# Thirteen chunks' combined weights finished ahead and kept in DRAM, and the first Strassen tile's x split on GpSimd: attention and two gated FFNs on one core

## The chip, the core and the metric

One core of a Trainium2 chip. The engines are TensorE (PE, whose weight loads are PEld), VectorE (DVE), ScalarE (ACT), GpSimd (POOL) and SyncE (SP); here SP issues nearly all DMAs, in one queue, in order. The metric is the device time of one launch in microseconds (us).

## What is computed

```python
B, H, S, D = 4, 8, 576, 64          # 2304 tokens of 512
scores = where(mask, q @ k.T / 8, -1e9)   # heads 0-3: the last 32 keys; heads 4-7: every 32nd key
x = softmax(scores) @ v             # 2304 x 512
xn = x / sqrt(mean(x * x) + 1e-6) * rms_g
x = (silu(xn @ w1_gate) * (xn @ w1_val)) @ w1_out     # d_ff 1536
out = (silu(x @ w2_gate) * (x @ w2_val)) @ w2_out
```

The six weight matrices come as 64-bit floats, 512x1536 or 1536x512.

## The kernel before

**Numbers.** A float64 weight block ("raw", 512 KB of 32-bit words, L211) is made into fp32 on the chip: two ACT steps (L228 low word, L220 high word) and two DVE steps (L232, L237). Every matrix product is then made of three fp32r products (hi x hi, hi x lo, lo x hi), so each operand is split: an ACT cast gives hi (L244 for weights, L1024 for x), a subtraction gives lo (DVE L248 for weights, L1025 for x).

**Two stages.** The hidden dimension is cut into 12 chunks of 128 in each FFN. Stage A (to about 396 us) does the attention and chunks 0 to 5 of the first FFN ("plain", six token segments of 256 to 512 tokens; functions `gate`, `hidden`, `down`). Stage B does chunks 6 to 11 of the first FFN and all of the second in five passes: chunks (6,7,8), (9,10,11), then (0-3), (4-7), (8-11). Each pass walks three supertiles of 768 tokens; gate and value products of a chunk are one 2x2 Strassen-Winograd product, of seven matrix products in place of eight.

**Strassen's operands.** For each supertile x is loaded (`stage_x`), and POOL forms four sums (L1008) and seven lo parts (L1025), two halves each. For the weights of a chunk `combined_step` (L268) loads gate and value blocks, decodes both, lets POOL form four differences of 128x256 (`sums`, L283, written into the raw buffer), and splits four parts into hi and lo.

**Places and order.** A finished chunk takes three of the 4 KB-per-partition places in `room[4]` and one 2 KB place in `room[2]`; there are three raw buffers. The list `late` holds the weight steps of stage B in order. `prefetch` starts the next one when its places are free, and `weights` lets `pace["op"]` of its operations go out at each point of the main program. Every engine runs its instructions in the order in which a scheduler issues them; `behind("act")` (L313) puts a weight operation behind the last ACT instruction of the main chain.

**The ACT chain of stage B.** Of the seven products the epilogue copies some from PSUM by ACT: `keep` (L1053, tile t), `seed` (L1059), silu (L1067); DVE adds (L1063, L1073), and ACT casts the hidden value (L1077). PE's next product goes into the bank that `keep` or `seed` has just emptied. At the end of stage A the program runs `plainpiece` (the last two down products) among the first Strassen products, and before that it stages the first supertile with `sum_x` and `split_q` on DVE.

Of the kernel before, what the change touches and what calls it, by code (L numbers as in the profile page):

```python
# [8 lines left out]
F32 = mybir.dt.float32  # L9
# [12 lines left out]
PRIO_W = -150  # L22
# [3 lines left out]
def attn_ffn_ffn(ctx: ExitStack, tc: tile.TileContext, q, k, v, w1g, w1v, w1o, rms_g, w2g, w2v, w2o, out):  # L26
# [58 lines left out]
    wq = []  # L85
    state = {"start": True, "hold": False, "kind": "", "lag": 3, "wait": 4}
# [41 lines left out]
    def prefetch(force=False):  # L128
        if late and (late[0].ready() or force) and not wq:
            st = late.pop(0)  # L130
            phase(st, 0)
            st.at, st.lag = clock[0], state["wait"]
            begun.append(st)
# [19 lines left out]
    def point():  # L153
        advance()
        weights()
# [45 lines left out]
    raws = [3]  # L201

    def fetch(m, c, z):
        raws[0] -= 1
# [5 lines left out]
        r = dec.tile([128, KC, 256], U32, tag="raw", name="raw", bufs=3)  # L210
        nc.sync.dma_start(out=r, in_=src)  # L211
        words = r.rearrange("p k f -> p (k f)").rearrange("p (n s) -> p n s", s=2)
        return {"raw": r, "lw": words[:, :, 0], "hw": words[:, :, 1]}

    def scale(cell, free=1):

        def high():
            cell["h"] = dec.tile([128, 512], F32, tag="dh", name="dh")
            with behind("act"):
                nc.scalar.activation(out=cell["h"], in_=cell["hw"].bitcast(F32), func=AF.Copy, scale=2.0 ** -112)  # L220

# [28 lines left out]
    def weight_step(m, c, z):  # L250
        cell = {}

        def load():
            cell["at"] = take((m, c, z == 2), 4)
            cell.update(fetch(m, c, z))
# [10 lines left out]
        return Step([load] + scale(cell) + [first, second], lambda: room[4] and raws[0] >= 1, PRIO_W)  # L266

    def combined_step(m, c):  # L268

        g, v = {}, {}  # L270
        at = []

        def load():
            at.extend([take((m, c, False), 4) for _ in range(3)] + [take((m, c, False), 2)])
            g.update(fetch(m, c, 0))
            v.update(fetch(m, c, 1))

        def sums():
            t = g["raw"].rearrange("p k f -> p (k f)").bitcast(F32).rearrange("p (a n) -> p a n", a=4)
# [4 lines left out]
            flat = t.rearrange("p a n -> p (a n)")  # L284
            g["parts"] = [(g["h"], 512, at[0]), (v["h"][:, 256:512], 256, at[3]), (flat[:, 0:512], 512, at[1]), (flat[:, 512:1024], 512, at[2])]
            g["t"] = []

        def first(i):
            def f():
                src, w, place = g["parts"][i]  # L290
                t = home(place, w, f"w{m}_{c}_{i}")
                g["t"].append(t)
                hi(t, src)
            if i == 2:
                f.late = True
            return f

        def second(i):
            def f():
                lo(g["t"][i], g["parts"][i][0])  # L300
                if i == 3:
                    raws[0] += 1
                    tg, tb, t12, t34 = g["t"]
                    wt[m, c, 0] = {1: tg[:, :, 0:256], 2: tg[:, :, 256:512], 3: tb, 5: t12[:, :, 0:256], 6: t12[:, :, 256:512],
                                   7: t34[:, :, 0:256], 4: t34[:, :, 256:512]}
                    wdone.add((m, c, 0))
            return f

        return Step([load] + scale(g, 0) + scale(v) + [sums] +
                    [f(i) for i in range(4) for f in (first, second)],  # L310
                    lambda: len(room[4]) >= 3 and room[2] and raws[0] >= 2, PRIO_W)

# [563 lines left out]

    segs = [(1, *e, 0, HC) for e in early]
# [17 lines left out]
    for key in (1, 0):  # L895
# [8 lines left out]
    late += [combined_step(1, c) if z == "c" else weight_step(1, c, 2) for z, c in  # L904
             (("c", 6), ("c", 7), ("d", 6), ("c", 8), ("d", 7), ("d", 8), ("c", 9), ("d", 9), ("c", 10), ("d", 10), ("c", 11), ("d", 11))]
    late += [combined_step(2, c) if z == "c" else weight_step(2, c, 2) for z, c in
# [38 lines left out]

    for si, (m, t0, n, c0, c1) in enumerate(segs):
        nxt = segs[si + 1] if si + 1 < len(segs) else None
# [6 lines left out]
        for c in range(c0, c1):  # L954
# [6 lines left out]
            if att and not steps and not active_att():  # L961
# [3 lines left out]
                open_pool("x7", "x7", 0, bufs=1)  # L965
                open_pool("wpb", "wpb", 0, bufs=1)
                open_pool("ob", "ob", 512, bufs=4)
                room[4] += [(pools["wpb"][0], f"v{i}") for i in range(2)]
# [19 lines left out]
    HN = 384  # L988
# [7 lines left out]
    xq = {}  # L996
# [194 lines left out]
    for n, (m, cs, t0) in enumerate(work):  # L1191
# [51 lines left out]
        pace["op"] = 1.0 if m == 2 else 0.7 if n else 1.4  # L1243
# [7 lines left out]
        for i, c in enumerate(chunks[:-1]):  # L1251
# [9 lines left out]
            if i == k - 2:  # L1261
                pace["op"] = 0.35 if n else 1.2
# [61 lines left out]
```

## Time and profile before

| what | value |
|---|---|
| three runs, us | 1048.94, 1049.05, 1049.20 (median 1049.05) |
| profiled execution, us | 1045.34 |
| its span, us | 1043.6 |
| mean granted TensorE clock | 0.974 |
| PE / PEld / DVE / ACT / POOL busy, us | 986.6 / 898.8 / 577.7 / 576.2 / 447.4 |
| DMA, MB | 133.85 |

Busy time is summed over the span, whatever the engine's stage; a row "idle before <- releaser" says how long an engine stood and what its wait ended with. Times of rows are from the start of the span. A matmul's own duration overlaps its neighbours': the pace of PE is seen in the distance of starts.

### The profile page before, as it was taken

The numbers are of one execution on the slowest core, as the hardware profiler recorded it, in microseconds if no ns is written. First come the engines' busy times: TensorE is split into PE (matmuls) and PEld (weight loads), VectorE is DVE, ScalarE is ACT, GpSimd is POOL, SyncE is SP. The second block draws the span as 40 slices with busy tenths as digits, with TensorE's granted clock in tenths as the row PEclk, the third lists the DMA queues.
The fourth block names the chain that finished last, engine by engine and source line by source line (L and its number), as shares of the span: only waits on it lengthen the run. The fifth ranks groups of instructions, "written<-read, shape, count | busy, mean of one in ns | idle before, by whom it ended". The sixth has DMA issues, their size and how long they took to land.

```text
span 1043.6 us, 16443 instructions
## 1 busy us (share of the span) xinstructions
PE 986.6 (95%) x5804; PEld 898.8 (86%) x5804; DVE 577.7 (55%) x1311; ACT 576.2 (55%) x1435; POOL 447.4 (43%) x463
## 2 busy tenths in 40 slices
PE   5758999999999997999999999999989999999998
PEld 4648998788789886899999999999988999899997
DVE  3779445454353677644766467433766337663433
ACT  5888646545623567555556467454766346563531
POOL 3312102103100061865696594743848164844500
PEclk9658999999999999999999999999999999999999
DMA  7675242251132256535736534403374342615021
GB/s 188 168 225 149 67 135 75 75 136 35 41 101 91 86 177 216 156 107 162 232 102 211 182 105 166 161 1 122 122 241 138 115 143 71 224 49 182 33 80 61
DMA packets 130090, 133.85 MB, mean 128 GB/s; under 512 B 41428, under 2 KB 113820, under 8 KB 130008
## 3 DMA queue, kind: packets, MB, share of 16 engines
q1 hardware_dynamic: 129816, 132.53, 39.9%
q8 instruction: 45, 0.74, 0.3%
q0 software_dynamic: 192, 0.28, 0.1%
q14 instruction: 37, 0.30, 0.1%
HBM read 99.75 MB, written 33.03 MB: 127 GB/s over the span
## 4 chain that ended last, share of the span: by engine, by line
PE 68%; POOL 10%; DVE 7%; DMA 7%; issue 4%; ACT 3%; SPq 1%; POOLq 0%; DVEq 0%; ACTq 0%
PE b_y L66 27%; PE b_a L66 15%; PE b_g L66 12%; PE b_v L66 11%; POOL xl L1025 5%; POOL raw L283 2%; PE b_a L69 2%; DMA raw<-in_moe_w_out_dram 2%; DVE w L248 2%; POOL xst L1008 1%; DMA raw<-in_moe_w_val_dram 1%; DMA raw<-in_moe_w_gate_dram 1%; DVE dh L237 1%; ACT dh L220 1%; SPq L383 1%
## 5 line engine op out<-in xcount | busy, mean ns | idle before, releaser
L1025 POOL TENSOR_TENSOR xl<-xst,xh 128x384 fp32r<-128x384 f32 x168 | 177.0, 1083 | 68.1 <-PE b_y L66 36.7
L66 PE MATMUL b_y<-xh,w 128*128 128x384 f32 x700 | 189.3, 336 | 5.5 <-ACT t L1053 5.5
L66 PE MATMUL b_g<-xh,w 128*128 128x384 f32 (+2 forms) x496 | 149.6, 349 | 7.2 <-ACT t L1053 4.5
L66 PEld LDWEIGHTS b_y<-xh,w 128*128 128x128 f32 x700 | 128.1, 188 | 9.0 <-ACT t L1053 7.1
L66 PE MATMUL b_v<-xh,w 128*128 128x384 f32 (+2 forms) x432 | 128.4, 347 | 4.3 <-ACT b_v L1059 2.7
L66 PE MATMUL b_a<-xh,w 128*128 128x384 f32 (+2 forms) x460 | 125.6, 336 | 0.8 <-ACT t L1053 0.7
L66 PE MATMUL b_y<-hh,w 128*128 128x256 f32 (+2 forms) x432 | 117.2, 342 | 1.0 <-ACT hh L800 1.0
L66 PE MATMUL b_y<-xl,w 128*128 128x384 f32 x350 | 117.7, 336 | 0.0
L66 PEld LDWEIGHTS b_g<-xh,w 128*128 128x128 f32 x496 | 91.7, 193 | 15.5 <-ACT t L1053 6.1
L1024 ACT CAST xh<-xst 128x384 fp32r<-128x384 f32 x180 | 85.9, 521 | 23.6 <-POOL xst L1008 20.4
L543 POOL TENSOR_TENSOR e<-e,rc 128x384 f32<-128x384 f32 (+3 forms) x40 | 38.0, 955 | 132.3 <-DVE rc L537 75.5
L283 POOL TENSOR_TENSOR raw<-dh 128x256 f32<-128x256 f32 x36 | 32.7, 928 | 141.6 <-DVE dh L237 106.3
L66 PEld LDWEIGHTS b_v<-xh,w 128*128 128x128 f32 x432 | 78.1, 188 | 12.6 <-ACT b_v L1059 3.5
L66 PEld LDWEIGHTS b_a<-xh,w 128*128 128x128 f32 x460 | 83.4, 188 | 5.1 <-ACT t L1053 1.3
L66 PE MATMUL b_g<-xl,w 128*128 128x384 f32 (+2 forms) x248 | 84.5, 341 | 2.6 <-POOL xl L1025 2.6
L66 PEld LDWEIGHTS b_y<-hh,w 128*128 128x128 f32 x432 | 77.2, 189 | 7.2 <-ACT hh L800 1.4
L66 PE MATMUL b_a<-xl,w 128*128 128x384 f32 (+2 forms) x230 | 77.2, 336 | 0.0
L66 PE MATMUL b_y<-hl,w 128*128 128x256 f32 (+2 forms) x216 | 72.6, 336 | 0.2 <-DVE hl L801 0.2
L66 PE MATMUL b_v<-xl,w 128*128 128x384 f32 (+2 forms) x216 | 72.6, 336 | 0.0
L1008 POOL TENSOR_TENSOR s<-xst 128x384 f32<-128x384 f32 x28 | 29.4, 1071 | 90.7 <-DMA xst<-y_d 53.6
L526 ACT ACTIVATE e<-e,nb 128x96 f32<-128x96 f32 (+2 forms) x152 | 56.3, 373 | 20.3 <-DVE nb L517 20.2
L66 PEld LDWEIGHTS b_y<-xl,w 128*128 128x128 f32 x350 | 65.8, 188 | 1.8
(204 smaller groups left out, 2195.7 us busy)
## 6 DMA issues: line engine op xcount, KB each, us to landing
xst<-y_d SPq DMA_DIRECT2D x18, 768.0 KB
raw<-in_moe_w_gate_dram SPq DMA_DIRECT2D x24, 512.0 KB
raw<-in_moe_w_val_dram SPq DMA_DIRECT2D x24, 512.0 KB
raw<-in_moe_w_out_dram SPq DMA_DIRECT2D x24, 512.0 KB
part<-ob SPq DMA_DIRECT2D x48, 256.0 KB
ob<-part SPq DMA_DIRECT2D x36, 256.0 KB
ob<-part SPq DMA_DIRECT2D x32, 192.0 KB
part<-ob SPq DMA_DIRECT2D x24, 192.0 KB
```

The costliest lines, as they stand in the source:

```text
L66: traced(nc.tensor.matmul(out_, a, b_, start=start, stop=stop, **how))
L69: traced(nc.tensor.transpose(out_, a, one))
L220: nc.scalar.activation(out=cell["h"], in_=cell["hw"].bitcast(F32), func=AF.Copy, scale=2.0 ** -112)
L237: nc.vector.scalar_tensor_tensor(out=h, in0=h, scalar=3, in1=cell["r"], op0=ALU.logical_shift_left, op1=ALU.bitwise_or)
L248: nc.vector.tensor_tensor(out=t[:, 1], in0=src, in1=t[:, 0].bitcast(F32), op=ALU.subtract)
L283: nc.gpsimd.tensor_tensor(out=t[:, z], in0=a, in1=b, op=ALU.subtract)
L383: engs[h].dma_start(out=t[0:108, h].rearrange("p (g d) -> p g d", d=D), in_=s)
L526: r = nc.scalar.activation(out=e[:qn, i, :kn], in_=e[:qn, i, :kn], func=AF.Exp, bias=nb[:qn, i:i + 1], scale=-1.0, accum_out=sums[:qn, i:i ...
L543: eng.tensor_tensor(out=e[:qn, :nt, :kn], in0=e[:qn, :nt, :kn], in1=rc[:qn, :nt].unsqueeze(2).to_broadcast([qn, nt, kn]), op=ALU.mult)
L1008: eng.tensor_tensor(out=out_[:, kk], in0=a[:, kk], in1=b[:, kk], op=op)
L1024: nc.scalar.copy(out=xh[:, kk], in_=src[:, kk])
L1025: eng.tensor_tensor(out=xl[:, kk], in0=src[:, kk], in1=xh[:, kk].bitcast(F32), op=ALU.subtract)
```

## The change

**Parking.** Thirteen of the eighteen chunks of stage B (first FFN 9, 10, 11; second 0, 1, 2, 3, 5, 6, 7, 9, 10, 11) are decoded, combined and split in their raw and "dh" buffers, without a place: hi parts go into the value block's dead raw buffer, lo parts over their sources. Each of the four parts is then stored to DRAM (two DMAs a part, eight a chunk), and the chunk is read back with four DMAs when its places are free. The last cast of a parked chunk overwrites the buffer that its first store reads. Chunks 6, 7, 8 of the first FFN and 4, 8 of the second go the old way. All of a chunk's stores and loads are on SP: 596 rows on that queue stand against 421, and 13 chunks write 23.9 MB and read 23.9 MB (1.835 MB each way a chunk).

**Where parks run.** Parks use the attention stage's three raw buffers at first, so that the parks of chunks 9 and 10 of the first FFN start in the first token segment; between the end of the attention and the last segment a pool "st" gives five raw and five dh buffers.

**First x.** `first_x` stages the first supertile in 128x384 pieces in 14 DMAs (3 before), and issues its 22 sums and lo parts one by one during the last plain segment, on POOL (before: 22 on DVE).

**Paces.** `pace["op"]` in stage B was 1.0 for the second FFN, 0.7 for the first, 1.4 for the first supertile, and 0.35 or 1.2 from the last chunk but one on; it becomes 0.6 (1.0, then 0.8, in the first supertile).

```diff
-    def combined_step(m, c):
+    def combined_step(m, c, how):
...
         def sums():
-            t = g["raw"].rearrange("p k f -> p (k f)").bitcast(F32).rearrange("p (a n) -> p a n", a=4)
+            flat = g["raw"].rearrange("p k f -> p (k f)").bitcast(F32)
+            t = flat.rearrange("p (a n) -> p a n", a=4)
...
+            spaces = v["raw"].rearrange("p k f -> p (k f)").bitcast(F32)
+            src = {0: g["h"], 1: flat[:, 0:512], 2: flat[:, 512:1024], 3: b22}
+            his = {0: spaces[:, 0:512], 1: spaces[:, 512:1024], 2: spaces[:, 0:512], 3: v["h"][:, 0:256]}
+            for i in (0, 3, 1, 2) if how != "park" else (0, 1, 3, 2):
...
+        def save(qs, a, hi_, lo_, t_):
+            w = 256 * len(qs)
+            d = dp.tile([128, 2, w], F32, name=f"pk{m}_{c}_{t_}")
+            nc.sync.dma_start(out=d[:, 0], in_=hi_.bitcast(F32))
+            nc.sync.dma_start(out=d[:, 1], in_=lo_.bitcast(F32))
+            parked.setdefault((m, c), {})[t_] = d
...
+    def recall_step(m, c):
+        def load():
+            got = {}
+            for i, qs in enumerate(QUARTERS):
+                w = 256 * len(qs)
+                t = home(take((m, c, False), 4 if w == 512 else 2), w, f"w{m}_{c}_{i}")
+                nc.sync.dma_start(out=t.bitcast(F32), in_=parked[m, c][i])
...
+        return Step([load], lambda: len(parked.get((m, c), ())) == 4 and len(room[4]) >= 3 and room[2], PRIO_W)
...
-    late += [combined_step(1, c) if z == "c" else weight_step(1, c, 2) for z, c in
-             (("c", 6), ("c", 7), ("d", 6), ("c", 8), ("d", 7), ("d", 8), ("c", 9), ("d", 9), ("c", 10), ("d", 10), ("c", 11), ("d", 11))]
...
+    plan("p19 p110 c16 d16 c17 c18 d17 d18 r19 d19 r110 d110 p111 p20 r111 d111 p21 r20 d20 r21 d21 p22 p23 r22 d22 r23 d23 "
+         "c24 d24 p25 p26 p27 r25 d25 r26 d26 r27 d27 c28 d28 p29 p210 p211 r29 d29 r210 d210 r211 d211")
...
+    def first_x():
...
+            def g():
...
+                with behind("act"):
+                    nc.scalar.copy(out=h[i][:, kk], in_=f[nm, kk])
+                nc.gpsimd.tensor_tensor(out=l[i][:, kk], in0=f[nm, kk], in1=h[i][:, kk].bitcast(F32), op=ALU.subtract)
...
     for si, (m, t0, n, c0, c1) in enumerate(segs):
+        if nxt_last(si):
+            while begun:
+                operate(begun[0])
+            racks.pop(0)
+            close_pools("st")
+            open_pool("x7", "x7", 0, bufs=1)
+            first_x()
...
-    cell = stage_x(1, 0)
-    sum_x(cell, nc.vector)
-    for i in (1, 2, 6, 5, 7, 4, 3):
-        split_q(cell, i, 0, nc.vector)
-        split_q(cell, i, 1, nc.vector)
...
-        pace["op"] = 1.0 if m == 2 else 0.7 if n else 1.4
+        pace["op"] = 0.6 if n else 1.0
...
-                pace["op"] = 0.35 if n else 1.2
+                pace["op"] = 0.6 if n else 0.8
```

In the plan "c" is a chunk combined as before, "p" one that is parked, "r" its recall, "d" the chunk's down weight (loaded and split as before). PE's order is the same, instruction for instruction, but for the weight tiles' names. Three places of the other engines' order follow (line numbers differ between the two programs: L1053 and L1210 are both `keep`, L244 and L251 the cast of a plain weight, L358 that of a combined one).

ACT in the second FFN's first supertile, around the copies t of one gate bank; `w_2_*` and `w_3_*` are weights of chunks 2 and 3 of that FFN. Before:

```order
L1067 ACTIVATE t_6964<-b_v 128x384
L244 CAST w_2_2_6970<-raw 128x512
L1053 COPY t_6975<-b_g 128x384
L220 ACTIVATE dh<-raw 128x512
L244 CAST w_2_3_6988<-raw 128x512
L1053 COPY t_7016<-b_g 128x384
L244 CAST w_3_0_7019<-dh 128x512
L1059 COPY b_a_7029<-b_a_7021 128x384
```

After:

```order
L1224 ACTIVATE t_7141<-b_v 128x384
L1210 COPY t_7150<-b_g 128x384
L251 CAST w_3_2_7166<-dh 128x512
L1210 COPY t_7187<-b_g 128x384
L1216 COPY b_a_7197<-b_a_7190 128x384
L1224 ACTIVATE b_g<-b_g 128x384
L1234 CAST hh<-b_g 128x384
```

Between the two copies the decode step into dh and the cast of raw are gone, and one cast of a down weight stands there.

POOL in the first supertile of the pass over chunks 9, 10, 11 (s is a sum of the next x, raw<-dh the weights' differences, xl the lo parts). Before:

```order
L1025 TENSOR_TENSOR xl<-s_5428,xh 128x384 x2
L283 TENSOR_TENSOR raw<-dh,raw 128x256
L1025 TENSOR_TENSOR xl<-xst,xh 128x384
L1008 TENSOR_TENSOR xst<-xst 128x384
L1025 TENSOR_TENSOR xl<-xst,xh 128x384 x5
L283 TENSOR_TENSOR raw<-dh,raw 128x256
L1025 TENSOR_TENSOR xl<-xst,xh 128x384
L1008 TENSOR_TENSOR s_5850<-xst 128x384 x2
L1008 TENSOR_TENSOR xst<-xst 128x384 x2
L283 TENSOR_TENSOR raw<-dh 128x256 x2
L283 TENSOR_TENSOR raw<-dh,raw 128x256 x2
L1025 TENSOR_TENSOR xl<-xst,xh 128x384
```

After:

```order
L1182 TENSOR_TENSOR xl<-s_5565,xh 128x384 x2
L1165 TENSOR_TENSOR xst<-xst 128x384
L1182 TENSOR_TENSOR xl<-xst,xh 128x384 x7
L326 TENSOR_TENSOR raw<-dh 128x256 x2
L326 TENSOR_TENSOR raw<-dh,raw 128x256 x2
L1165 TENSOR_TENSOR s_5986<-xst 128x384 x2
L1165 TENSOR_TENSOR xst<-xst 128x384 x2
L1182 TENSOR_TENSOR xl<-xst,xh 128x384
```

The weights' differences leave the run of lo parts and stand in one block ahead of the next sums s.

ACT and SP at the end of the first token segment (sg is the sigmoid part of silu, hh the hidden cast, ss and sq the squares of the norm, e the softmax, xraw the next segment's x). ACT before:

```order
L663 ACTIVATE ss<-x_1156 128x576
L672 ACTIVATE sq<-x_1156 128x288 x2
L526 ACTIVATE e,sums<-e,nb 128x96 x2
L789 ACTIVATE sg<-b_g 128x256
L76 COPY pT<-b_a_1565 96x512
L800 CAST hh<-sg 128x256
```

ACT after:

```order
L358 CAST raw<-dh 128x512
L755 ACTIVATE ss<-x_1190 128x576
L764 ACTIVATE sq<-x_1190 128x288 x2
L358 CAST dh<-dh 128x256
L618 ACTIVATE e,sums<-e,nb 128x96 x2
L358 CAST raw<-raw 128x512
L905 CAST xh<-xraw 128x256 x2
L358 CAST raw<-raw 128x512
L881 ACTIVATE sg<-b_g 128x256
L76 COPY pT<-b_a_1641 96x512
L892 CAST hh<-sg 128x256
```

SP after, from the last four stores of chunk 9 on:

```order
L370 DMA pk_9_3_1170<-dh 128x256
L371 DMA pk_9_3_1170<-dh 128x256
L370 DMA pk_9_2_1194<-raw 128x512
L371 DMA pk_9_2_1194<-raw 128x512
L218 DMA raw<-in_moe_w_val_dram 128x4x256
L865 DMA xraw<-x_d_1_994 128x2x256
L475 DMA vs_1613<-in_v_dram 108x1x320 x4
L477 DMA vs_1613<-in_v_dram 18x4x128
L865 DMA xraw<-x_d_1_994 128x2x256
L370 DMA pk_10_0_1382<-raw 128x512
```

All four casts of chunk 10's park and the casts of xraw stand ahead of the last sg of the segment; on SP the value block of chunk 10 and the next segment's xraw stand behind the stores of chunk 9. Before, xraw (L773) was issued right after the third weight load of chunk 5, ahead of qn and kn.

## Rows read from the trace of the kernel before

**Rows 1.** The page's first part: busy time, share, instructions.

```profile
PE 986.6 (95%) x5804; PEld 898.8 (86%) x5804; DVE 577.7 (55%) x1311; ACT 576.2 (55%) x1435; POOL 447.4 (43%) x463
```

**Rows 2.** Waits of PE, 385 to 430 us, the four longest: total, times, longest.

```profile
PE b_v L66 <- ACT b_v L1059: 2.7, 1, 2.7
PE b_g L66 <- ACT t L1053: 1.2, 2, 0.9
PE b_v L66 <- ACT t L1067: 1.1, 2, 0.7
PE b_y L66 <- ACT hh L800: 1.0, 1, 1.0
```

**Rows 3.** Waits of PE, 505 us to the end.

```profile
PE b_y L66 <- ACT t L1053: 5.5, 5, 1.9
PE b_g L66 <- ACT t L1053: 3.3, 3, 1.7
PE b_g L66 <- POOL xl L1025: 2.6, 1, 2.6
PE b_a L66 <- ACT t L1053: 0.3, 1, 0.3
```

**Rows 4.** Timeline of ACT, 618 to 624 us: start, duration, line, step, idle before.

```profile
617.78 0.48 ACT L1053 COPY t<-b_g 128x384 f32<-128x384 f32 x1
622.01 0.66 ACT L220 ACTIVATE dh<-raw 128x512 f32<-128x512 f32 x1 [3.75 <-POOL raw L283]
...
623.09 0.47 ACT L1053 COPY t<-b_g 128x384 f32<-128x384 f32 x1
```

**Rows 5.** Timelines of SP and ACT, 391 to 400 us.

```profile
392.07 0.38 SPq L211 DMA_DIRECT2D raw<-in_moe_w_val_dram  x1
...
397.64 0.65 ACT L228 ACTIVATE raw<-raw 128x512 uint32<-128x512 uint32 x1 [2.19 <-DMA raw<-in_moe_w_val_dram]
...
398.70 0.47 ACT L1059 COPY b_v<-b_g 128x384 f32<-128x384 f32 x1
```

**Rows 6.** Busy time by stretch, 505 to 540 us: PE, PEld, DVE, ACT, POOL, PEclk, DMA share, GB/s.

```profile
505.00:510.00 5.00, 5.00 (x31) 5.00 (x30) 1.89 (x4) 3.10 (x7) 5.00 (x6) 1.00 0.97 312
...
530.00:535.00 5.00, 4.06 (x14) 4.06 (x15) 1.33 (x2) 4.47 (x10) 4.92 (x5) 0.66 0.35 105
```

**Rows 7.** Timelines of SP, ACT and PE, 92 to 136 us: the last segment-0 steps.

```profile
93.33 8.68 SPq L773 DMA_DIRECT2D xraw<-x_d  x4
...
96.39 0.70 ACT L813 CAST xh<-xraw 128x256 fp32r<-128x256 f32 x2
...
114.96 0.41 ACT L800 CAST hh<-sg 128x256 fp32r<-128x256 f32 x1
...
121.97 0.41 ACT L800 CAST hh<-sg 128x256 fp32r<-128x256 f32 x1 [1.37 <-DVE sg L797]
...
127.27 0.36 ACT L789 ACTIVATE sg<-b_g 128x256 f32<-128x256 f32 x1
...
129.19 0.41 ACT L800 CAST hh<-sg 128x256 fp32r<-128x256 f32 x1 [0.59 <-DVE sg L797]
...
129.24 0.38 PE L66 MATMUL b_y<-hh,w 128*128 128x256 f32 x1
```

**Rows 8.** The page's groups of instructions on POOL: busy, mean ns, idle before.

```profile
L1025 POOL TENSOR_TENSOR xl<-xst,xh 128x384 fp32r<-128x384 f32 x168 | 177.0, 1083 | 68.1 <-PE b_y L66 36.7
L283 POOL TENSOR_TENSOR raw<-dh 128x256 f32<-128x256 f32 x36 | 32.7, 928 | 141.6 <-DVE dh L237 106.3
L1008 POOL TENSOR_TENSOR s<-xst 128x384 f32<-128x384 f32 x28 | 29.4, 1071 | 90.7 <-DMA xst<-y_d 53.6
```

**Rows 9.** The groups of instructions on DVE, 340 to 405 us: its lo parts of x.

```profile
L1025 DVE TENSOR_TENSOR xl<-xst,xh 128x384 fp32r<-128x384 f32 x12 | 6.3, 548 | 6.2 <-ACT xh L1024 6.2
```

**Rows 10.** Busy time by stretch, 345 to 396 us, columns as in rows 6.

```profile
345.00:375.00 30.00, 30.00 (x145) 25.27 (x145) 24.13 (x46) 18.30 (x38) 7.81 (x7) 1.00 0.40 133
375.00:396.00 21.00, 19.74 (x88) 16.00 (x87) 16.49 (x23) 13.53 (x24) 9.70 (x10) 1.00 0.43 137
```

More of the change, by code (lines that the diff above doesn't have):

```diff
@@ L154, in point @@
         advance()
+        if eager:
+            eager.pop(0)()
         weights()
@@ L199, in wait, with fetch @@
         pass
-    raws = [3]
-    def fetch(m, c, z):
-        raws[0] -= 1
+    rack = {"pool": dec, "free": 3, "bufs": 3, "dh": 2}
+    racks = [rack]
+    parked = {}
+    def fetch(m, c, z, cell):
+        bk = cell["bk"] = racks[0]
+        bk["free"] -= 1
         w = WSRC[m][z].bitcast(U32)
@@ L283, in sums @@
                 nc.gpsimd.tensor_tensor(out=t[:, z], in0=a, in1=b, op=ALU.subtract)
[L284 to L311, printed above, removed]
+            spaces = v["raw"].rearrange("p k f -> p (k f)").bitcast(F32)
@@ new lines, in sums @@
+            src = {0: g["h"], 1: flat[:, 0:512], 2: flat[:, 512:1024], 3: b22}
+            his = {0: spaces[:, 0:512], 1: spaces[:, 512:1024], 2: spaces[:, 0:512], 3: v["h"][:, 0:256]}
+            for i in (0, 3, 1, 2) if how != "park" else (0, 1, 3, 2):
+                w = 256 * len(QUARTERS[i])
+                if how == "park":
+                    parts.append((QUARTERS[i], src[i], his[i].bitcast(F32R), src[i].bitcast(F32R), i))
+                    continue
+                if how == "split" and i == 1:
+                    places = [(q_, src[i][:, 256 * j:256 * j + 256], at[n4 + 1 + j]) for j, q_ in enumerate(QUARTERS[i])]
+                    places = [((q_,), a, p) for q_, a, p in places]
+                else:
+                    places = [(QUARTERS[i], src[i], at[n4] if i == 3 else at[min(i, n4 - 1)])]
+                for qs, a, place in places:
+                    t_ = home(place, 256 * len(qs), f"w{m}_{c}_{qs[0]}")
+                    parts.append((qs, a, t_[:, 0], t_[:, 1], t_))
@@ new lines, in op, with g_, first @@
+        def op(i, f):
+            def g_():
+                f(*parts[i])
+                if i == len(parts) - 1 and f is (save if how == "park" else second):
+                    g["bk"]["free"] += 1
+                    if how == "park":
+                        v["bk"]["free"] += 1
+                    else:
+                        wt[m, c, 0] = got
+                        wdone.add((m, c, 0))
+            return g_
+        def first(qs, a, hi_, lo_, t_):
+            with behind("act"):
+                nc.scalar.copy(out=hi_, in_=a)
@@ new lines, in second @@
+        def second(qs, a, hi_, lo_, t_):
+            with behind("dve"):
+                nc.vector.tensor_tensor(out=lo_, in0=a, in1=hi_.bitcast(F32), op=ALU.subtract)
+            if how != "park":
+                for j, q_ in enumerate(qs):
+                    got[q_] = t_[:, :, 256 * j:256 * j + 256]
+        def save(qs, a, hi_, lo_, t_):
[4 more added lines that the diff above has]
+            parked.setdefault((m, c), {})[t_] = d
@@ new lines, in combined_step, with recall_out @@
+        k = 5 if how == "split" else 4
+        lag = 1 if how == "park" else 2
+        ops = [op(i, f) for i in range(k) for f in ((first, second, save) if how == "park" else (first, second))]
+        ops[lag * (3 if how == "park" else 2)].late = True
+        return Step([load] + scale(g, 0) + scale(v, int(how != "park")) + [sums] + ops, ready, PRIO_W)
+    def recall_out(m, c):
+        def load():
+            t = home(take((m, c, True), 4), 512, f"w{m}_{c}_2")
+            nc.sync.dma_start(out=t.bitcast(F32), in_=parked[m, c, 2])
+            wt[m, c, 2] = t
+            wdone.add((m, c, 2))
+        return Step([load], lambda: (m, c, 2) in parked and room[4], PRIO_W)
```

115 lines of the change are left out of this document (99 added, 16 removed), and 3 rows, old and new, of the table att.

## The prediction

> **What bounds the kernel now.** First the page's busy times: PE works 986.6 us of a span of 1043.6, every other engine under 600 [rows 1]. The work of PE is not touched (its order is the same), so only its idle time and its clock can change: 57 us at most, the start of the attention among it, where nothing is changed.
>
> Then the waits of PE, by stretch, since a share over the whole span hides them. In the transition to Strassen the four longest come to 6.0 us, 2.7 of it for the `seed` copy [rows 2]. From 505 us to the end PE waits nine times on a `keep` copy (5.5 + 3.3 + 0.3 = 9.1 us) and once on a lo part from POOL (2.6) [rows 3]. That is all.
>
> Then why `keep` is late, from ACT's timeline. At 622 us two copies stand 5.3 us apart, and between them ACT stood still for 3.75 us: the decode step into dh waited for POOL's weight differences, and the copy that PE needs stood behind it in ACT's order [rows 4]. ACT was not busy; it stood behind the wrong instruction. The `seed` copy is the same kind: a weight block issued on SP at 392.07 is first used at 397.64, 5.57 us later, ACT stood for it, and the copy came at 398.70 [rows 5].
>
> Last, the clock: from 530 to 535 us the granted clock is 0.66, so part of the stretch ran at the lower of the two levels, 1.2 and not 2.4 GHz, right after one of the stalls; PE started 14 products in 4.06 busy us, against 31 in 5 at full clock [rows 6]. At full pace 4.06 us make 25; 11 products at 0.16 us are missing, 1.8 us.
>
> So at stake are 6.0 + 9.1 + 2.6 + 1.8 = 19.5 us.
>
> **The change, part by part.** *The nine keep waits, -8.1 us.* With parking, most supertiles of the later passes have no combined decode of their own. At 622 us the order now has one cast of a down weight between the two copies, and that waits on DVE only, not on POOL; where a chunk is still combined, POOL's differences stand ahead of the sums s, not among the lo parts. POOL reached them late because lo parts of 1.08 us each [rows 8] stood ahead. I take away 9.1 and leave 1.0 for casts that wait for the moved differences. The bounds: nothing is left (-9.1), or only the places where no combined decode remains gain, a third of the sum (-3). The new paces only shift these operations in the order, and are counted with it.
>
> *The lo part from POOL, -2.6 us.* It was late since the differences of the weights came between POOL's lo parts. In the new order all four differences of the chunk stand ahead of the run. Bounds -2.6 and 0.
>
> *The clock, -1.8 us.* It fell after a stall that goes. Bounds -1.8 and 0: I can't show that the stall made it fall.
>
> *The transition, -4 us of 6.0.* The decode of chunks 9 and 10 leaves 392 to 427 us, so nothing just issued is waited for ahead of `seed`; but a decode of chunk 11 now stands in the same stretch, and the last cast of chunk 8, ahead of `seed`, waits for POOL. I leave 2.0 us for these. Bounds -6.0 and 0.
>
> *First x on POOL, 0.* 14 lo parts at 1.08 us and 8 sums at 1.07 are 23.7 us on POOL [rows 8]; on DVE a lo part took 0.548 us, so all 22 some 12.1 us [rows 9]. POOL is busy for 7.8 and 9.7 us from 345 to 396 [rows 10], so 17.5 becomes 41.2 of 51; DVE's 24.1 and 16.5 fall by 12. I cost it at nothing because x is used first after 396 us and POOL has 10 us to spare. The cover is thin; if it goes, what is late is chunk 8's four differences (0.93 us each [rows 8]), then its cast, then `seed`. SP issues 11 DMAs more for it, at some 0.38 us each [rows 5], 4 us of a queue that then has only results to store. The Trainium skill ("GPSIMD Engine Reference", section 3.1, Elementwise) says that VectorE stays the rule for elementwise work, with a tensor_tensor 1.96 times as long on GpSimd; here it is 1083 against 548 ns, 1.98 times, so the ratio agrees. By that rule the move would be a loss, by the rows of POOL's idle time none; it is the third rival below.
>
> *The stores, recalls and the SP queue, +2 us.* 104 stores and 52 loads add 47.7 MB. At the 312 GB/s that the queue reached in a full stretch [rows 6] that is 153 us of transfer in over 900, beside PE's work. The order has the recalls ahead of their use by some 40 us or more of PE's work, and one recall of 1.835 MB takes 5.9 us at that pace. What they do cost: SP waits for a free place ahead of the next store of results or load of x, and ACT's casts wait for stores to land. None of these is in the trace. Below, 0 (all hidden); above, two blocks' landings of the length seen, 5.57 us [rows 5], less the part that ACT has free: 4. I take the middle.
>
> *The parks in segment 0, +3.5 us.* This is the cost that the order shows plainly. Until now the next segment's x was issued at 93.33 and cast from 96.39 on, far ahead of need [rows 7]; three waits now stand in ACT's order in front of copies that PE needs. (1) The last cast of chunk 9 waits for a store to land, some 3 us after its issue by the nearest row, xraw's 3.06 us from issue to cast [rows 7]. Its first part was stored some 7 us before, ahead of the hidden cast of 114.96 [rows 7]: nothing. (2) Chunk 10's value block stands on SP behind all eight stores of chunk 9; the last lands at about 119 us (its cast just ahead of the hidden cast of 114.96, lo at 116, 3 us to land), the block 3.06 to 5.57 us later [rows 7, 5], at 122 to 124.6, and ACT's decode steps for it stand ahead of the hidden cast that came at 121.97 before [rows 7]. (3) Chunk 10's last cast stands ahead of the sigmoid of 127.27 and waits for POOL: block at 124, decoded by 126.5, four differences of 0.93 us, 130.2, cast 130.8. The sigmoid then is at 131, 3.5 us late. It has no slack: its hidden cast starts at 129.19 and PE's first product with it at 129.24 [rows 7]. The waits overlap, as (3) contains (2). Bounds: 0, if the blocks land early and PE's other work fits; 9 (3.06 + 5.57), if two landings lie on PE's path in full.
>
> The sum: -8.1 - 2.6 - 1.8 - 4 + 0 + 2 + 3.5 = -11.0 us. The profiled execution took 1045.34 us, 3.7 below the median of the three runs; I take the sum from the median: 1049.05 - 11.0 = **1038**.
>
> **The rivals.** *(a) The waits change their name.* ACT still runs in order, and all casts of parks and of down weights still go on it; chunks 4 and 8 of the second FFN are still combined beside Strassen, and one cast of each parked chunk waits for a store. For it: ACT's stalls come from any late step ahead of `keep`, not from POOL alone. Against: between 618 and 624 us nothing is left that waits on POOL. Then 3 of the 9.1, 2.6 and half the transition (2) are won, the clock stays, and 5.5 is paid: about 1047; with the transition and the clock won, 1043. Range 1043 to 1048.
>
> *(b) Slower: the parks of chunks 9 and 10 in segment 0 hold up the chain of segment 1.* SP is in order: if ACT is late, its store is late, so the value block behind it is late, so ACT is later still, and xraw behind them too; each turn costs a landing. Three turns at 5.57 us are 16.7, and a stall of that length may cost the clock as at 530 us, 1.8. That replaces the 3.5: -14.5 + 18.5 = +4, 1053. It decides against the change once this stretch costs over 17 us, or over 8 if half of the gains fail too. For it: no slack at 129.24 us [rows 7]. Against: ACT has idle time around those steps and PE can start other products there.
>
> *(c) GpSimd is the bound in the last segment.* If its 23.7 us come ahead of chunk 8's differences, the transition gains nothing, and `seed` is later by up to the 11.6 us that POOL takes longer than DVE: 1038 + 4 + (0 to 11.6) is 1042 to 1054. That is what the skill's rule on elementwise work would make of it. Against: 10 us of slack.
>
> *(d) Recalls come late.* PE would wait for the DMA itself, at some 5.9 us a chunk where the queue is full [rows 6]; two of them would give 1050. Against: the distance in the order.
>
> **How the numbers follow.** A measurement of this kernel can tell about 0.2%, 2.1 us, from no change: faster is under 1046.95, slower over 1051.15. My forecast (1030 to 1043) has 0.58; (a) 0.22, of which four fifths are faster and the rest the same; (b) 0.10, nearly all slower; (c) 0.06, a third each; (d) 0.04, half faster or the same, half slower. Faster: 0.58 + 0.17 + 0.02 = 0.77, less a little for the forecast's worst bounds together: 0.75. Slower 0.14, same 0.11. The forecast's own low end: all gains and no cost would be 1029.6, so 1030. The high end takes in (a), part of (c) and (d): 1050. Left out are (b) and the tails, near 0.17.
>
> **What would show it.** Right: PE's waits on `keep` from 505 us on fall from 9.1 us to about 1, ACT has no wait on POOL's raw ahead of it, the wait on xl is gone, the clock is 1.0 around 530 us, and new waits of PE on hh or sg of 2 to 5 us stand between 115 and 135 us. Wrong: waits of the same length under another name (ACT on DMA, w on POOL), PE waiting on w from a recall, a wait for `seed` of over 2 us with POOL busy through 396 us, or a stretch from 115 to 135 us that is over 10 us longer.

## The result, and the profile after

The changed kernel took 1060.72 us (median of 6 runs, 1058.73 to 1063.92) against 1049.12 us of the kernel before on the same chips (6 runs): a ratio of 1.0104, 95% interval 1.0073 to 1.0136. It is slower, by about what it was forecast to be faster. The profiled execution has a span of 1056.9 us, 13.3 more than the one before.

The page's busy times, which answer to [rows 1]; PE's work did not grow by 13 us:

```profile
PE 992.2 (94%) x5804; PEld 905.4 (86%) x5804; DVE 589.0 (56%) x1289; ACT 575.5 (54%) x1435; POOL 472.9 (45%) x485
```

Since PE's order is the same in all kernels of this study, the k-th product of one can be set against the k-th of another. The table has how much later PE gets (us; + is time lost) in each stretch of the kernel before, worked out from the starts of the 5804 products in each kernel's one profiled execution; the last column is the sum.

| kernel | to 110 | 110-160 | 160-385 | 385-395 | 395-430 | 430-540 | 540-570 | 570-645 | 645-815 | 815-end | sum |
|---|---|---|---|---|---|---|---|---|---|---|---|
| after | +1.6 | +13.7 | -0.3 | +5.2 | -5.6 | -1.1 | +7.6 | -2.4 | -5.6 | 0.0 | +13.1 |
| e1_hold | +3.3 | -0.1 | +2.7 | +5.5 | -6.0 | +0.8 | +5.2 | -2.4 | -5.6 | +0.5 | +3.9 |
| e2_dvex | +8.2 | +17.1 | -0.3 | -0.6 | -5.1 | +1.0 | +5.2 | -2.4 | -5.5 | +0.4 | +17.9 |
| e3_poolx | +2.7 | +0.1 | -0.3 | +6.2 | +0.5 | -0.5 | +1.3 | 0.0 | +1.7 | -0.1 | +11.7 |
| e4_nopark | +4.2 | +0.1 | -0.3 | +6.3 | -0.7 | +0.7 | +3.6 | -0.6 | +0.7 | +3.8 | +17.8 |
| e5_both | +7.2 | +0.3 | +2.2 | +0.3 | -5.1 | +0.8 | +5.3 | -2.4 | -5.6 | +0.1 | +3.2 |
| e6_late | +3.1 | +2.8 | +7.6 | +1.0 | -6.0 | +1.1 | -0.7 | +1.1 | -0.3 | -0.2 | +9.5 |
| e7_pace | +4.5 | +0.2 | -0.3 | 0.0 | -2.7 | +0.7 | +3.5 | -0.4 | -0.7 | +3.8 | +8.6 |
| e8_xq | +7.7 | +14.9 | -0.3 | +5.3 | -6.7 | +0.4 | +5.9 | -2.4 | -5.6 | -0.2 | +19.0 |
| e9_one | +3.2 | +3.4 | -0.3 | +5.8 | -5.9 | -0.9 | +8.0 | -2.4 | -5.7 | -0.2 | +5.0 |
| e10_p1late | +0.4 | 0.0 | +2.2 | -0.5 | -5.1 | +0.8 | -0.7 | +0.7 | -5.6 | +0.1 | -7.7 |
| e11_seg2 | +8.6 | +0.2 | +2.3 | -0.5 | -5.1 | -0.3 | -0.7 | +1.8 | -5.7 | -1.1 | -0.4 |
| e12_recall | +3.9 | +14.7 | -0.3 | +5.3 | -4.4 | +0.9 | +5.7 | -2.4 | -5.6 | -1.2 | +16.7 |

The first row shows three losses (13.7, 5.2 and 7.6 us) and gains of 14.7 us in four stretches. The first column isn't put down to the change: it varies by as much between executions in which all engines have the same order up to 100 us (last section).

**The first loss, 13.7 us: x of segment 1.** Waits of PE from 110 to 150 us; the kernel before has none listed from 105 to 140 us (xh and xl are the hi and lo part of x):

```profile
PE b_g L66 <- ACT xh L905: 7.0, 1, 7.0
PE b_a L69 <- issue: 2.3, 1, 2.3
```

ACT's timeline in the same stretch (start, duration, step, idle before):

```profile
120.12 0.62 ACT L358 CAST raw<-raw 128x512 fp32r<-128x512 f32 x1 [3.60 <-DMA pk<-raw]
...
138.51 0.71 ACT L905 CAST xh<-xraw 128x256 fp32r<-128x256 f32 x2 [3.92 <-DMA xraw<-x_d]
```

SP's timeline:

```profile
102.37 0.37 SPq L218 DMA_DIRECT2D raw<-in_moe_w_gate_dram  x1
...
123.21 0.38 SPq L218 DMA_DIRECT2D raw<-in_moe_w_val_dram  x1
123.85 0.37 SPq L865 DMA_DIRECT2D xraw<-x_d  x1
130.38 3.07 SPq L475 DMA_DIRECT2D vs<-in_v_dram  x4
...
134.07 0.38 SPq L865 DMA_DIRECT2D xraw<-x_d  x1
```

The second half of x was issued at 134.07 and cast at 138.51, and PE stood 7.0 us for it; before, x was issued from 93.33 us on [rows 7], and its last cast began at 99.5. Where x could have had its buffer, at 102.37 (e9), the gate block of chunk 10 went out instead, into the third of the three raw buffers that x shares with the weights. Later the second half stood on SP behind loads of v, which waited for PE (waits of SP, 115 to 145 us):

```profile
SPq L475 <- PE b_a L66: 6.1, 1, 6.1
```

The 2.3 us come from the cast of chunk 9 behind its store. The profile names no releaser ("issue"), but ACT's copies out of the bank b_a, behind that cast, end at 122.04, and PE's next product into it starts at 122.14. After each of the two stalls products ran at the lower level, which by their starts cost some 1.5 us each time; the last 1 us of the 13.7 is in steps too short to be put down to anything. Busy time by stretch, columns as in [rows 6]:

```profile
120.00:125.00 5.00, 2.87 (x18) 2.61 (x18) 2.82 (x14) 4.14 (x15) 0.26 (x1) 0.72 0.47 166
...
135.00:140.00 5.00, 1.03 (x3) 0.86 (x4) 2.33 (x8) 1.33 (x3) 0.78 (x1) 0.58 0.96 310
140.00:145.00 5.00, 5.00 (x44) 4.77 (x43) 1.84 (x4) 1.65 (x4) 0.00 (x0) 0.73 0.53 178
```

The granted clock of these stretches is 0.58 to 0.73, so a part of each ran at 1.2 GHz.

**The second loss, 5.2 us: hh at the end of stage A.** Waits of PE, 397 to 440 us, where [rows 2] were:

```profile
PE b_y L66 <- ACT hh L892: 3.7, 1, 3.7
PE b_y L66 <- DVE hl L893: 1.7, 1, 1.7
```

No wait for `seed` is left, nor for `keep` or silu (hl is the lo part of the hidden value). But ACT stood for a down weight ahead of hh. Timelines of POOL (the last lo part of the first x), SP (`w<-pk` is a piece of a recall) and ACT:

```profile
392.39 1.40 POOL L1081 TENSOR_TENSOR xl<-xst,xh 128x384 fp32r<-128x384 f32 x1 [0.62 <-ACT xh L1080]
...
396.22 0.56 SPq L397 DMA_DIRECT2D w<-pk  x1
396.83 1.22 SPq L1159 DMA_DIRECT2D xst<-x_d  x2
398.10 0.62 SPq L397 DMA_DIRECT2D w<-pk  x1
400.77 0.34 SPq L218 DMA_DIRECT2D raw<-in_moe_w_out_dram  x1
...
408.35 0.67 ACT L235 ACTIVATE raw<-raw 128x512 uint32<-128x512 uint32 x1 [3.88 <-DMA raw<-in_moe_w_out_dram]
```

The block took 7.6 us from issue to use, behind the second supertile's x and two pieces of a recall. Here too the clock fell:

```profile
410.00:415.00 5.00, 2.67 (x6) 1.78 (x7) 4.97 (x7) 2.86 (x6) 1.92 (x2) 0.50 0.85 283
```

By the starts of the products this cost some 2.4 us, a part of it in the table's next column.

**The third loss, 7.6 us: a park's lo part on DVE.** Waits of PE from 515 us to the end, which answer to [rows 3]:

```profile
PE b_a L66 <- DVE t L1220: 5.5, 1, 5.5
PE b_y L66 <- ACT t L1210: 4.0, 4, 2.9
PE b_y L66 <- DVE hl L1235: 0.7, 1, 0.7
PE b_g L66 <- DVE hl L1235: 0.2, 1, 0.2
```

`keep` fell from 9.1 to 4.0 us and the wait on xl is gone. A new one, for DVE's add (L1220), took 5.5 us. POOL's and DVE's timelines around it:

```profile
576.32 1.94 POOL L1165 TENSOR_TENSOR s<-xst 128x384 f32<-128x384 f32 x2 [6.57 <-DMA xst<-x_d]
578.21 0.72 POOL L326 TENSOR_TENSOR raw<-dh,raw 128x256 f32<-128x256 f32 x1
...
578.97 1.47 DVE L362 TENSOR_TENSOR dh<-dh,raw 128x512 fp32r<-128x512 f32 x1 [8.28 <-POOL raw L326]
580.36 0.54 DVE L1220 TENSOR_TENSOR t<-t,b_a 128x384 f32<-128x384 f32 x1
```

A park writes its lo part over the source (`dh<-dh,raw`), which the last difference of POOL still reads; that difference stood behind the sums s, and s waited for x. DVE is in order, so the add waited for a load it has nothing to do with. That load was not slower than before: POOL's timeline of the kernel before has the same wait for x, with nothing of PE's behind it:

```profile
561.84 2.44 POOL L1008 TENSOR_TENSOR s<-xst 128x384 f32<-128x384 f32 x2 [6.99 <-DMA xst<-x_d]
```

The clock fell after this stall as well, which cost some 2.3 us:

```profile
575.00:580.00 5.00, 0.45 (x3) 0.13 (x1) 1.03 (x1) 0.47 (x1) 3.68 (x5) 0.96 0.52 177
580.00:585.00 5.00, 4.04 (x13) 4.05 (x14) 3.15 (x7) 1.41 (x3) 3.31 (x3) 0.50 0.28 105
```

### The profile page after: what moved, and what is told of

The parts are those of the page before. It is cut to its first block, busy times and chain, and to the rows that moved or that the text cites. A ratio compares the mean times of both kernels' runs of the same rounds, so it can differ in the third digit from the quotient of the medians.

```text
span 1056.9 us, 16819 instructions
## 1 busy us (share of the span) xinstructions
PE 992.2 (94%) x5804; PEld 905.4 (86%) x5804; DVE 589.0 (56%) x1289; ACT 575.5 (54%) x1435; POOL 472.9 (45%) x485
## 5 line engine op out<-in xcount | busy, mean ns | idle before, releaser
L1182 POOL TENSOR_TENSOR xl<-xst,xh 128x384 fp32r<-128x384 f32 x168 | 185.6, 1136 | 70.9 <-PE b_a L66 42.8
L1181 ACT CAST xh<-xst 128x384 fp32r<-128x384 f32 x168 | 80.2, 522 | 12.5 <-POOL xst L1165 12.4
L66 PE MATMUL b_y<-w,hh 128*128 128x512 f32 x216 | 67.1, 392 | 0.0
```

Source lines behind the costliest of these rows:

```text
L66: traced(nc.tensor.matmul(out_, a, b_, start=start, stop=stop, **how))
L1181: nc.scalar.copy(out=xh[:, kk], in_=src[:, kk])
L1182: eng.tensor_tensor(out=xl[:, kk], in0=src[:, kk], in1=xh[:, kk].bitcast(F32), op=ALU.subtract)
```

## The experiments

The theory: three separate losses, each at one place. The rivals: the traffic of stores and recalls as such; GpSimd; the paces. A time is the median, and the ratio that to the kernel before on the same chip, with its interval.

**e1_hold: the parks wait for segment 1.**

```diff
-        if late and (late[0].ready() or force) and not wq:
+        if state["go"] and late and (late[0].ready() or force) and not wq:
...
         xs = xs_of.pop(si)
+        state["go"] = si >= 1
```

> The changed kernel, but no late weight step starts before the second token segment has begun, so the parks of chunks 9 and 10 no longer take the attention's raw buffers in segment 0. Theory (the parks hold the next segment's x: the second half of xraw was issued at 134.07 us and PE stood 7.0 us for it, after 2.3 us for a cast that waited for a store, with the clock at 0.58 to 0.73 around; PE is 14.1 us late by 140 us): the stretch from 115 to 145 us goes back to the pace of the kernel before, the rest stays, 1060.7 - 14 = about 1047 (1045 to 1052, since the parks now meet the x of segment 2). Rival (the 47.7 MB of extra traffic on one queue cost the time, wherever it lies): the loss moves to where the parks now run, 1057 to 1061.

Measured: 1049.93 us, ratio 1.0002 (0.9971 to 1.0033). The stretch from 110 to 160 us went from +13.7 to -0.1; 2.7 us came back at the next segment (160 to 385). The bytes are the same, so traffic as such is not the cause of this loss.

**e2_dvex: the first x on VectorE again.**

```diff
-            first_x()
...
+    cell = stage_x(1, 0)
+    sum_x(cell, nc.vector)
+    for i in (1, 2, 6, 5, 7, 4, 3):
+        split_q(cell, i, 0, nc.vector)
+        split_q(cell, i, 1, nc.vector)
     def plainpiece(js, si, c, h):
```

> The changed kernel with the first supertile's x staged and split on VectorE as before; the parks stay. Theory (at 407 us ACT stood 3.9 us for a down weight's load, issued at 400.77 and landed at 408.35, beside recalls and x loads; POOL had nothing to do with it): the time stays near 1060 (1057 to 1064), with the wait ahead of seed perhaps back for 1 to 3 us. Rival (GpSimd's slower split is what made the end of stage A late): the 5.2 us at 407 go, 1053 to 1056.

Measured: 1062.52 us, ratio 1.0119 (1.0069 to 1.0168). The number is the theory's, and the theory is wrong all the same: at 385 to 395 us the loss went from +5.2 to -0.6. The total hides it, as this execution lost 6.6 us more before 110 us and 3.4 more up to 160. From here on the places are read, not the totals.

**e3_poolx: the kernel before with only the first x on GpSimd.**

```diff
+        if si == len(segs) - 1:
+            open_pool("x7", "x7", 0, bufs=1)
+            first_x()
...
-    cell = stage_x(1, 0)
-    sum_x(cell, nc.vector)
-    for i in (1, 2, 6, 5, 7, 4, 3):
-        split_q(cell, i, 0, nc.vector)
-        split_q(cell, i, 1, nc.vector)
```

> The kernel before with only the first supertile's x split piece by piece on GpSimd; no parks, old order and paces of the weights. Theory (GpSimd has the time): the end of stage A loses nothing, 1047 to 1051. Rival (the slower engine delays the differences of chunks 7 and 8, and through them ACT): PE waits 3 to 8 us more between 390 and 400 us, 1052 to 1057.

Measured: 1057.52 us, ratio 1.0067 (1.0036 to 1.0099): the rival. PE's longest wait from 385 to 430 us:

```profile
PE b_y L66 <- ACT hh L803: 6.2, 1, 6.2
```

Without any park hh is 6.2 us late. How, the timelines of SP and ACT show:

```profile
383.04 1.91 SPq L1052 DMA_DIRECT2D xst<-x_d  x3
385.61 0.39 SPq L214 DMA_DIRECT2D raw<-in_moe_w_val_dram  x1
...
392.81 0.68 ACT L231 ACTIVATE raw<-raw 128x512 uint32<-128x512 uint32 x1 [3.56 <-DMA raw<-in_moe_w_val_dram]
```

and the waits of SP, 375 to 412 us, have what held the x load:

```profile
SPq L1052 <- POOL xl L980: 2.5, 1, 2.5
```

The next x is loaded only when POOL has made the last lo part; so it is issued at 383 us (364.43 before), just ahead of a value block, which then needs 7.2 us. GpSimd was not full, as POOL's timeline has it idle for 6.37 us until that x landed: what counts is the moment at which its last step frees a load.

**e4_nopark: all chunks kept, in the old list's order; new paces, new part order and first x on GpSimd stay.**

```diff
-    plan("p19 p110 c16 d16 c17 c18 d17 d18 r19 d19 r110 d110 p111 p20 r111 d111 p21 r20 d20 r21 d21 p22 p23 r22 d22 r23 d23 "
...
+    plan("c16 c17 d16 c18 d17 d18 c19 d19 c110 d110 c111 d111 c20 d20 c21 d21 c22 c23 d22 d23 "
+         "c24 d24 c25 c26 c27 d25 d26 d27 c28 d28 c29 c210 c211 d29 d210 d211")
```

> The changed kernel with all eighteen chunks combined and kept as before (no stores, no recalls), in the old order; first x on GpSimd, new paces and new order of a chunk's parts stay. Theory (parks alone bring both the gains at the passes' starts and the losses in segment 0 and at 575 us): the losses of 14.1 and 8.3 us go and most of the 13 us of gains go with them, 1045 to 1051, with waits of PE on the keep copies again from 505 us on. Rival (the new paces and part order, not the parks, took the keep waits away): 1034 to 1040.

Measured: 1062.94 us, ratio 1.0118 (1.0065 to 1.0171): neither. The loss at 110 us is gone, that of hh stays (+6.3), new ones stand at 540 to 570, 645 to 815 and from 815 on (+3.6, +0.7, +3.8), while the keep waits at 760, 770 and 905 us are gone without a park. So the paces have a part in the gains, which e7 takes alone.

**e5_both: e1 and e2 together** (both diffs above).

> The parks held until segment 1 and the first x on VectorE, together; everything else as in the changed kernel. Theory (two separate losses, the second being that with GpSimd's split the second supertile's 1.5 MB of x is loaded some 10 to 19 us later, right ahead of a weight block that ACT waits for in front of hh): the gain of the first, 1049.9, less the 4.7 us that the stretch from 390 to 430 us was better with x on VectorE: 1045 (1043 to 1048), no wait of PE on hh over 1 us around 400 us. Rival (the late block at 400 us comes from the recalls alone): 1049 to 1051.

Measured: 1043.92 us, ratio 0.9934 (0.9906 to 0.9963), faster than before; 385 to 395 us is at +0.3, and PE's wait for hh is 1.3 us (1.0 before). The recalls still stand in that stretch, but x was loaded at 373.65, and the down weight takes 3.9 us from issue to use, not 7.6 (timelines of SP and ACT):

```profile
373.65 1.89 SPq L1159 DMA_DIRECT2D xst<-x_d  x3
...
394.37 0.33 SPq L218 DMA_DIRECT2D raw<-in_moe_w_out_dram  x1
...
398.28 0.67 ACT L235 ACTIVATE raw<-raw 128x512 uint32<-128x512 uint32 x1 [0.21 <-DMA raw<-in_moe_w_out_dram]
```

With e3, where x was late and nothing was recalled, this shows that the split on GpSimd makes hh late, and that recalls without it don't. That it acts through the late x load is read from the timelines; no run moves that load alone.

**e6_late: e5, and every park's first cast ten points later.**

```diff
         ops[lag * (3 if how == "park" else 2)].late = True
+        if how == "park":
+            ops[0].late = True
```

> As the kernel with both edits, and a parked chunk's first cast goes out ten points later after its differences. Theory (at 575 us DVE stood 8.3 us for POOL's differences of a parked chunk, because the lo part of a park is written over a source that the last difference reads, and that difference stood behind sums waiting for x; the add that PE needs was behind it): that wait of 4 to 5.5 us and its lower clock go, 1045 - 5.8 = about 1039 (1037 to 1043). Rival (the DMA queue is full at 565 to 575 us, so another step waits in its place): 1044 to 1047.

Measured: 1054.5 us, ratio 1.0028 (0.999 to 1.0065). In neither range. The wait at 540 to 570 us went (-0.7), as said, but other parks got late: +7.6 at 160 to 385, where x of segment 2 is held longer, and the gain of 645 to 815 fell from 5.6 to 0.3.

**e7_pace: the kernel before with the new paces.**

```diff
-        pace["op"] = 1.0 if m == 2 else 0.7 if n else 1.4
+        pace["op"] = 0.6 if n else 1.0
...
-                pace["op"] = 0.35 if n else 1.2
+                pace["op"] = 0.6 if n else 0.8
```

> The kernel before with only the new paces of the weight operations in the Strassen stage (0.6; 1.0 and 0.8 in the first supertile). Theory (from the run without parks: the paces, not the parks, took away the late keep waits and the late lo part of 762, 770, 806 and 906 us, 7.7 us in all, and the parks are what makes the slower pace possible): those four are gone, while weights of some chunks come late, with new waits of PE in products with hh: 1045 to 1056, by the size of the second. Rival (the new order of a chunk's parts did it): the four waits stay, 1047.5 to 1051.

Measured: 1051.38 us, ratio 1.0016 (0.9988 to 1.0044). The longest waits of PE, 500 to 1050 us:

```profile
PE b_g L66 <- DVE hl L1078: 2.0, 1, 2.0
PE b_y L66 <- ACT w L244: 1.8, 2, 1.6
PE b_g L66 <- ACT w L244: 1.8, 2, 1.6
PE b_y L66 <- DVE w L248: 1.4, 2, 1.1
...
PE b_a L66 <- ACT t L1053: 0.5, 1, 0.5
PE b_y L66 <- ACT t L1053: 0.4, 1, 0.4
```

`keep` is at 0.9 us instead of 9.1, and xl is gone, by the paces alone. In their place PE waits for weights (w). So the slower pace clears ACT's order, and it is with the parks, in the changed kernel, that the waits for w are gone. Parks at the old paces were not run: what they do to `keep` by themselves stays open.

**e8_xq: the changed kernel, x of segment 1 on GpSimd's DMA queue.**

```diff
-                nc.sync.dma_start(out=x[:, :, o:o + w], in_=d[:, 2 * half:2 * half + 2, a:a + w])
+                (nc.gpsimd if m == 1 and t0 == segs[1][1] else nc.sync).dma_start(out=x[:, :, o:o + w], in_=d[:, 2 * half:2 * half + 2, a:a + w])
```

> The changed kernel with the x of segment 1 loaded from GpSimd's DMA queue instead of SyncE's; parks in segment 0 as they are. Theory (the second half of x had its buffer by about 124 us, but on SyncE it stood behind loads of v that waited 6.1 us for PE, and was issued at 134.07): it is issued by 127 us, PE's stall of 7.0 us at 132 us shrinks to under 2 and the one of 2.3 us at 120 stays; 8 to 9 us less, 1052 (1050 to 1056). Rival (the raw buffer comes free only with the stores of the parks, whatever the queue): 1058 to 1062.

Measured: 1062.38 us, ratio 1.0103 (1.0072 to 1.0134); 110 to 160 us is at +14.9. A miss: the second half went out at 139.43 us, behind POOL's differences, in an execution 7.7 us later by then. The edit put POOL's order in place of SP's, so it does not tell whether SP's order held x.

**e9_one: the changed kernel with one park, chunk 9, in segment 0.** `n` is the length of the list at the start.

```diff
-        if late and (late[0].ready() or force) and not wq:
+        if (state["go"] or len(late) == state["n"]) and late and (late[0].ready() or force) and not wq:
...
         xs = xs_of.pop(si)
+        state["go"] = si >= 1
```

> The changed kernel with only chunk 9's park in segment 0; chunk 10 waits for segment 1. The move to GpSimd's queue changed nothing, so the theory is now the raw buffers: with the gate block of chunk 10 in the third of three, x finds none until chunk 9's stores have landed; with one park it finds one or two. Theory: x of segment 1 is issued before 125 us and PE's 7.0 us at 132 us are gone with their low clock; the 2 to 4 us for the cast that waits for chunk 9's store stay; 9 us less than 1060.7, 1052 (1049 to 1055). Rival (one park is enough to hold the ACT order up): 1057 to 1062.

Measured: 1051.88 us, ratio 1.0017 (0.999 to 1.0044), in the theory's range; 110 to 160 us at +3.4. The longest wait of PE, 105 to 145 us:

```profile
PE b_a L69 <- issue: 2.0, 1, 2.0
```

and the issue of x in SP's timeline:

```profile
102.81 5.54 SPq L865 DMA_DIRECT2D xraw<-x_d  x2
```

The 7.0 us are gone, the 2 us for the store stay. Ahead of 102.81 SP waited for a step of DVE that frees a raw buffer (waits of SP, 97 to 104 us):

```profile
SPq L865 <- DVE dh L244: 4.5, 1, 4.5
```

In the changed kernel (97 to 103 us) the gate block of chunk 10 has that same wait, and so the buffer:

```profile
SPq L218 <- DVE dh L244: 4.5, 1, 4.5
```

So the buffer that this block took is what x lacked. The edit also takes chunk 10's casts and stores out of the segment; the wait of 7.0 us, though, ended with x's own cast.

**e10_p1late: e5, and the later first cast for chunk 1 of the second FFN alone.**

```diff
+        if (m, c) == (2, 1):
+            ops[0].late = True
```

> Parks from segment 1 on, first x on VectorE, and the later first cast for chunk 1 of the second FFN alone, the one parked at 565 to 580 us. Theory (delaying all parks brought new waits in segments 1 and 2 and at 605 to 740 us, delaying this one doesn't): the wait of 4.2 us for DVE's add at 568 us goes and nothing comes in its place: 1044 - 5.5 = 1038.5 (1036 to 1042). Rival (the differences of this park have to wait for x whatever follows them, and the next step of the chunk blocks ACT or DVE instead): 1043 to 1050.

Measured: 1039.34 us, ratio 0.9923 (0.9893 to 0.9953). The total is the theory's, but the place shows half of it: 540 to 570 us went from +5.3 to -0.7, while 570 to 645 us went from -2.4 to +0.7, so 2.9 us are gained and not 5.5. The rest of the distance to e5 lies where both kernels have the same order (the first 110 us alone differ by 6.8 us), and the intervals of e5, e10 and e11 overlap: which of the three is fastest is not shown. Its longest waits of PE from 385 us on:

```profile
PE b_y L66 <- ACT b_y L1218: 3.2, 1, 3.2
PE b_v L66 <- DVE t L1222: 2.4, 2, 2.1
PE b_y L66 <- ACT t L1212: 1.2, 3, 0.9
```

The 2.1 us are the theory's "nothing in its place" failing: three lo parts of the same park now stand in a row ahead of the next add (DVE, 569.49 us), the first of them still behind POOL:

```profile
565.53 1.49 DVE L362 TENSOR_TENSOR dh<-dh,raw 128x512 fp32r<-128x512 f32 x1 [2.31 <-POOL raw L326]
```

**e11_seg2: e10 with the parks from segment 2 on** (`si >= 2`).

> As the kernel before it in this list, with the parks held until segment 2. Theory (the 2.6 us lost at 165 to 180 us, where xraw of segment 2 is late, come from the same shared raw buffers): 2 to 3 us less than that kernel, 1036 (1033 to 1040). Rival (the parks meet the x of segment 3 in the same way, or chunks 6 to 8 come late for the end of stage A): the same time or more, 1039 to 1050.

Measured: 1042.64 us, ratio 0.9932 (0.9906 to 0.9957). The rival's range: 160 to 385 us is at +2.3, as in e10 (+2.2). But its reason does not show: from 105 to 395 us PE has no wait for xh or xl, its longest is 1.2 us for a copy of the attention, and the 2.3 us are spread over several short steps.

**e12_recall: the recalls held until stage A is issued.**

```diff
-        return Step([load], lambda: len(parked.get((m, c), ())) == 4 and
+        return Step([load], lambda: state["go"] and len(parked.get((m, c), ())) == 4 and
...
+    state["go"] = True
+
     def plainpiece(js, si, c, h):
```

> The changed kernel with the first recall, and what follows it in the list, held until stage A has been issued. Theory (the x load of the second supertile, moved by GpSimd's split to just ahead of a down weight's load, is what makes hh late at 407 us): PE's wait of 3.7 us on hh stays within 1.5 us; the time 1058 to 1064. Rival (the recalls' 1.8 MB in the same stretch are the cause): the wait is under 1.5 us, and the time 1054 to 1058.

Measured: 1063.93 us, ratio 1.0157 (1.0103 to 1.0211). Inconclusive: the scheduler put the recalls into the same place of SP's queue (the first at 399.58 us, between the pieces of x), so the edit moved nothing there, and the wait on hh stayed (3.8 us). What the recalls add to the late block when x is late too stays open.

## Why the prediction was wrong, point by point

The sum had -16.5 us of gains and +5.5 of costs. The profile has 14.7 of gains from 395 us on, less than 2 us from the forecast, and 26.5 us of losses (13.7 + 5.2 + 7.6): the costs were mis-sized, nearly fivefold. That the gains agree is in part luck, as their parts show.

- *The nine keep waits, -8.1, and the lo part, -2.6.* The waits named are gone: 9.1 us became 4.0, and 2.6 became none. The reason was wrong: I gave it to the parks, and e7 shows that the paces alone take these waits away, which I had counted as mere shifts. What the parks add is that weights are not late at that pace; of the runs here only those with both gain time from 505 us on. Of the 4.0 us, 2.9 are new: at 537 us PE waits for a copy where the kernel before had no wait. That is rival (a) in small, a wait under another name: ACT's decode step stood 4.96 us for a store (timeline of ACT after the change):

```profile
538.66 0.67 ACT L227 ACTIVATE dh<-raw 128x512 f32<-128x512 f32 x1 [4.96 <-DMA pk<-dh]
```

- *The clock, -1.8.* It left 530 us and came back after each new stall (granted clocks of 0.50 to 0.73 above). Worked out from the starts of the products, the lower level cost some 8 us in all, inside the three losses and the stretch after the second: the same term with the other sign.
- *The transition, -4.* The part after `seed` gained 5.6 us, inside the bounds. Of the reason, half is shown: the paces alone, without parks, gained 2.7 there (e7).
- *First x on POOL, 0.* Wrong by 5.2 to 6.2 us (the changed kernel, e3). I asked whether GpSimd had the time, and it had; I did not ask what its last step frees. That is rival (c) by its place and price, though not by its mechanism. The Trainium skill's rule that I set aside ("GPSIMD Engine Reference", section 3.1, Elementwise: leave elementwise work to VectorE) would have pointed the right way; the loss came through a load, not through GpSimd's busy time.
- *Stores, recalls and SP, +2.* One place alone cost 7.6 us, by a cause that isn't traffic: the lo part of a park is written in place and so waits for all of POOL's differences. The diff showed the in-place write; I never listed what DVE would stand behind. Moving one cast takes 6.0 us out of that stretch and brings 3.1 back right behind it (e5 to e10). A store made ACT late once (4.96 us, above), as the term had it.
- *The parks in segment 0, +3.5.* This step failed most, by 10.2 us. I followed ACT's waits for chunk 10 in detail and noted that x stood behind the stores on SP, but priced x at nothing. x lives in the same three raw buffers as the parks; its halves were issued at 123.85 and 134.07 instead of from 93.33 on, and PE's 7.0 us are the second one's landing. The hidden cast and the sigmoid that I priced are not among PE's waits there. Rival (b) had the place and the sign (18.5 us against 13.7 measured), and a chance of 0.10.

The forecast's own sign says the same: it called itself wrong if 115 to 135 us grew by over 10 us, and by the starts of the products this stretch grew by 13.3.

## What to carry to other kernels

Before work is moved earlier, list every other step that allocates from the same buffers, and give each of those loads a new issue time: a queue's order shows its place, not what the delay costs. When work goes to an idle but slower engine, the question is not its busy share but which load waits for its last step, and what that load then collides with. And where one engine's order is unchanged, set its starts side by side, place by place, before a total is believed.

## What the runs showed that was not expected

The first 110 us vary from execution to execution by up to 8 us: +0.4 us in e10 and +8.6 in e11, in which every engine has the same order up to 100 us. Busy time from 75 to 90 us, first of e10:

```profile
75.00:90.00 15.00, 13.63 (x90) 12.12 (x90) 13.18 (x61) 11.47 (x38) 3.26 (x3) 0.81 0.93 264
```

and of e11:

```profile
75.00:90.00 15.00, 12.60 (x58) 11.18 (x59) 11.30 (x40) 8.94 (x25) 2.24 (x2) 0.59 0.94 246
```

The granted clock stayed longer at 1.2 GHz in e11 (0.59 against 0.81), and 58 products were started instead of 90. What decides it no run here shows. It makes a single total of this kernel uncertain by several us: e11's 1042.64 against e10's 1039.34 is of that size.
